# Retention and two feed-forward layers on one core: state decay on R, a new lead-in order, bursts ahead of projections, split products for the first eight units

## The chip, the core and the metric

The kernel runs on one core of one Trainium2 chip. The metric is the device time of one execution in microseconds (us). The engines are named as the profile names them: PE (TensorE, matmuls), PEld (its weight loads), DVE (VectorE), ACT (ScalarE), POOL (GpSimd) and SP (the queue that issues most DMAs). Each engine takes its instructions in the order in which the program holds them; a wait at the head of a queue holds all that stands behind it.

## What is computed

```python
# retention: B, H, S, D = 4, 8, 768, 64
for t in range(S):
    state = gamma * state + k[t]^T v[t]          # per batch and head, 64 x 64
    y[t] = scale * (q[t] @ state)
x = y as (3072, 512)
h = x @ w_in                                     # 512 -> 2048
x = (h * sigmoid(1.702 * h)) @ w_out             # 2048 -> 512
x = (sigmoid(x @ w_gate) * (x @ w_val)) @ w_out2 # 512 -> 1536 -> 512
```

## The kernel before

**Retention** goes by chunks of 128 tokens, 24 in all, six to a batch (`c = s % 6`). For chunk `s`: `emit_scores` (L137) multiplies keys by queries into two PSUM banks and DVE multiplies them by the decay mask into `A` (L148); `emit_y` (L173) adds the state's part (L178, queries scaled on POOL into `qs`, L120, times `R`) and the chunk's own part (L185, `V` times `A`), then ACT rounds the bank into `xh` (L189) and DVE subtracts the rest into `xl` (L190); `emit_update` (L152) adds `K^T vs` to the state bank `st` (L165, `vs` scaled on POOL, L112) and ACT copies it to `R` (L171). The state is kept without decay from chunk to chunk, so the queries are scaled by a table `dq` per `c`, which ACT makes in the lead-in (`emit_decays`, L125).

**The first layer** has 2048 / 128 = 16 slices of features. A *unit* is one block of 512 tokens and one slice `f`. Its projection (`proj`, L256) is 12 matmuls of 128x512: the float32 product as three products of two float32r parts (`wh*xh`, `wh*xl`, `wl*xh`). ACT and DVE make the gated value (`gated`, L263); two units later (`DEPTH`) `emit_out` (L336) adds the unit to four accumulators. For the first eight units (`i < WHOLE`) that product is four plain float32 matmuls (L352), which the profile shows as eight rows, with the gated value and the weight unsplit; from unit 8 on it is 12 float32r matmuls, for which `split_w` (L248: ACT `wh`, POOL `wl`), a cast `gh` (L275) and a subtraction `gl` (L282) make the parts. Units 0 to 7 are the first half of block 0, 8 to 15 that of block 1.

**Weights** come as 64-bit floats and are converted on the core (`convert`, L209): ACT scales both words (`cva` L222, `cvb` L224), DVE joins sign and bits (L229, L232), POOL adds (L242, `wraw`). `cvb` has two buffers. In units 0 to 7 two tiles are converted in each unit: `conv` at the unit's head, `conv2` with its ACT part at the head and its DVE and POOL parts at the unit's end, after the gated value.

**The order** is written out by hand. A unit runs: both conversions' ACT part, `conv`, projection, split of the next unit's weights, gated value, a *burst* where the table `bursts` has one (`burst`, L298: `y` and state of a chunk, scores of the next, its POOL work and loads), `conv2`, then `emit_out` of the unit before last. Projections, `y` and scores of the bursts take PSUM banks in turn from one row of three (`h`, banks 4 to 6), so a burst's `y` bank is taken again by the next projection behind the burst's two score banks. In the lead-in (L648 to L699) chunks 0 to 3 go through `retain` one after another, with conversions between them, ahead of unit 0.

Of the kernel before, what the change touches and what calls it, by code (L numbers as in the profile page):

```python
# [8 lines left out]
F32 = mybir.dt.float32  # L9
# [15 lines left out]
def retention_moe_moe2(  # L25
# [20 lines left out]
    WARM = 10  # L46
# [29 lines left out]
    dq_sb = [const.tile([P, KC, C], F32, name=f"dq{i}") for i in range(CPB - 1)]  # L76
    dv_sb = const.tile([P, CPB - 1, H], F32, name="dv_sb")
    dc_sb = const.tile([P, H], F32, name="dc_sb")
    dg_sb = const.tile([P, KC], F32, name="dg_sb")
    sig = const.tile([P, 1], F32, name="sig")  # L80
    dm_sb = const.tile([P, 2, KC, C], F32, name="dm_sb")
# [8 lines left out]
    in_t = {}  # L90
# [14 lines left out]
    def emit_prep(s):  # L105

        c = s % CPB
        q, v = in_t[s][Q], in_t[s][V]
        vs = qs = None
        if c < CPB - 1:  # L110
            vs = at_p.tile([P, H, D], F32, name="vs", tag="vs")
            nc.gpsimd.tensor_tensor(  # L112
                out=vs,
                in0=v.rearrange("p (h d) -> p h d", h=H),
                in1=dv_sb[:, c, :].unsqueeze(2).to_broadcast([P, H, D]),
                op=ALU.mult,
            )
        if c:
            qs = at_p.tile([P, KC, C], F32, name="qs", tag="qs")
            nc.gpsimd.tensor_tensor(  # L120
                out=qs, in0=q.rearrange("p (a i) -> p a i", a=KC), in1=dq_sb[c - 1], op=ALU.mult
            )
        qs_t[s], vs_t[s] = qs, vs

    def emit_decays(c):  # L125

        for a in range(KC):
            nc.scalar.mul(dq_sb[c - 1][:, a, :], dq_sb[max(c - 2, 0)][:, a, :], dg_sb[:, a:a + 1])
# [23 lines left out]
    def emit_update(s):  # L152


        c = s % CPB
        if c == CPB - 1:
            return
        if c == 0:
            state[s // CPB] = psum_tile("st", (P, KC, P))
        st = state[s // CPB]  # L160
        kn, vs = in_t[s][KN], vs_t[s]
        for hp in range(KC):
            for i in range(2):
                h = 2 * hp + i
                nc.tensor.matmul(  # L165
                    st[D * i:D * (i + 1), hp, :D], kn[:, D * h:D * (h + 1)], vs[:, h, :],
                    start=(c == 0 and hp == 0), stop=True, skip_group_check=True,
                )
        for i in range(2):
            a, b = D * i, D * (i + 1)  # L170
            nc.scalar.copy(R[(s + 1) % 2][a:b, :, a:b], st[a:b, :, :D])  # L171

    def emit_y(s, xh, xl, o):  # L173
# [16 lines left out]
        nc.vector.tensor_tensor(out=xl[:, :, o:o + C], in0=bank, in1=xh[:, :, o:o + C], op=ALU.subtract)  # L190
# [98 lines left out]
    def retain(s):  # L289

        j, i = s // 4, s % 4
        if i == 0:
            alloc_x(j)
        emit_y(s, *x_t[j], i * C)
        emit_update(s)
        del in_t[s], qs_t[s], vs_t[s]

    def burst(s):  # L298

        retain(s)  # L300
        if s + 1 < NSTEP:
            emit_scores(s + 1)
            emit_prep(s + 1)
        load_next(s + 2, Q, K, V, KN)
# [343 lines left out]
    with tc.manual_schedule():  # L648
        load_in(0, Q, in_p, "in")
        load_in(0, K, in_p, "in", nc.scalar)  # L650
        nc.sync.dma_start(out=dm_sb, in_=decay.rearrange("p (i a j) -> p i a j", i=2, a=KC))
        nc.sync.dma_start(out=dv_sb[:, 0, :], in_=dv)
        load_in(0, V, in_p, "in", nc.scalar)
        load_in(0, KN, in_p, "in", nc.scalar)
        nc.sync.dma_start(out=dg_sb, in_=dg)
        nc.sync.dma_start(out=dc_sb, in_=dv[P // 2:P // 2 + 1, :].to_broadcast([P, H]))
        nc.sync.dma_start(out=dq_sb[0], in_=dq.rearrange("p (a i) -> p a i", a=KC))
        for t in range(1, 4):
            for i in (Q, K, V):
# [20 lines left out]
        emit_decays(1)  # L680
        banks.extend(["h", "acc", "h", "acc", "h", "acc", "acc"])
        emit_prep(0)
        emit_scores(0)
        load_next(4, KN, V)
# [18 lines left out]
        for i, (b, f) in enumerate(units):  # L703
# [194 lines left out]
```

## Time and profile before

| what | value |
|---|---|
| median of 3 runs | 1178.56 us (1177.11 to 1178.95) |
| the profiled execution's own time | 1178.58 us |
| its span from first to last instruction | 1176.8 us |
| mean granted clock of TensorE | 0.997 |
| PE busy | 1163.3 us (99% of the span) |
| DVE, ACT, POOL busy | 643.5, 578.5, 559.0 us |

The profiled execution stands at the median of the runs, and its time is its span and 1.8 us around it. PE is busy nearly throughout, so one reads first where it is not, and then which of its work can shrink. Most of that is in the first 60 us.

### The profile page before, as it was taken

The page shows a single profiled execution, that of the slowest core. Times are in us where ns is not written, and L with a number is a line of the kernel's source. Part 1 is how long each engine was busy: PE and PEld are TensorE (multiplying, and loading weights), DVE is VectorE, ACT ScalarE, POOL GpSimd, SP SyncE. Part 2 cuts the span into 40 slices and gives each one's busy share as a digit, 9 for nine tenths or more (in the row PEclk, how much of TensorE's full clock was granted, in tenths as well). Part 3 has the DMA queues.
Part 4 walks back from the last instruction along what each step waited for, and adds up shares of the span by engine and source line. Part 5 has one row for each costly group of instructions (what it writes and reads, how often), then busy time and mean ns, then how long its engine had stood idle before and what let it go on. Part 6 is the DMA issues. An engine that isn't in the chain of part 4 may idle for free.

```text
span 1176.8 us, 16048 instructions
## 1 busy us (share of the span) xinstructions
PE 1163.3 (99%) x5916; PEld 953.8 (81%) x5916; DVE 643.5 (55%) x878; ACT 578.5 (49%) x1016; POOL 559.0 (48%) x434
## 2 busy tenths in 40 slices
PE   7899999999999999999999999999999999999998
PEld 7666888888888888887888888888888888888887
DVE  4755455565455455554664626377626468636454
ACT  4645665455545555454554535264526164626250
POOL 3666774334433444433454616166616167625340
PEclk8999999999999999999999999999999999999999
DMA  8664345444354333403102202042202043212111
GB/s 296 230 221 141 107 144 189 161 152 129 105 152 153 117 117 126 143 28 106 29 1 94 77 27 81 27 152 99 81 27 81 27 143 107 75 35 73 36 36 72
DMA packets 62574, 123.47 MB, mean 105 GB/s; under 512 B 6816, under 2 KB 16288, under 8 KB 62496
## 3 DMA queue, kind: packets, MB, share of 16 engines
q1 hardware_dynamic: 61920, 121.54, 31.5%
q8 instruction: 46, 0.75, 0.3%
q10 hardware_dynamic: 576, 0.92, 0.2%
q14 instruction: 32, 0.26, 0.1%
HBM read 98.31 MB, written 24.12 MB: 104 GB/s over the span
## 4 chain that ended last, share of the span: by engine, by line
PE 95%; DVE 1%; ACT 1%; DMA 1%; POOL 1%; issue 0%; SPq 0%; DVEq 0%; POOLq 0%; ACTq 0%
PE pa L503 17%; PE pd L503 8%; PE h L261 7%; PE h L259 7%; PE h L260 7%; PE acc L356 7%; PE acc L358 7%; PE acc L357 7%; PE po L625 4%; PE po L627 4%; PE pb L503 4%; PE po L626 4%; PE acc L352 2%; PE h L144 2%; PE h L185 2%; PE pd L625 1%
## 5 line engine op out<-in xcount | busy, mean ns | idle before, releaser
L252 POOL TENSOR_TENSOR wl<-wraw,wh 128x512 fp32r<-128x512 f32 x112 | 151.7, 1360 | 274.6 <-ACT wh L251 258.7
L259 PE MATMUL h<-xh,wh 128*128 128x512 f32 x384 | 153.2, 399 | 1.8 <-DVE gw L270 1.5
L270 DVE TENSOR_TENSOR sg<-h,sg 128x512 f32<-128x512 f32 x88 | 60.8, 691 | 169.0 <-ACT sg L269 168.9
L261 PE MATMUL h<-xh,wl 128*128 128x512 f32 x384 | 149.8, 390 | 0.2
L260 PE MATMUL h<-xl,wh 128*128 128x512 f32 x384 | 149.6, 389 | 0.2 <-DVE xl L190 0.2
L356 PE MATMUL acc<-gh,wh 128*128 128x512 f32 x352 | 138.9, 395 | 0.0
L357 PE MATMUL acc<-gh,wl 128*128 128x512 f32 x352 | 137.1, 390 | 0.0
L358 PE MATMUL acc<-gl,wh 128*128 128x512 f32 x352 | 137.1, 390 | 0.0
L495 POOL TENSOR_TENSOR ol<-raw,oh 128x768 fp32r<-128x768 f32 x36 | 67.0, 1861 | 124.4 <-ACT oh L492 124.4
L251 ACT CAST wh<-wraw 128x512 fp32r<-128x512 f32 x184 | 107.7, 616 | 31.2 <-PE acc L358 31.0
L269 ACT ACTIVATE sg<-h 128x512 f32<-128x512 f32 x88 | 52.6, 597 | 131.0 <-PE h L261 130.7
L503 PE MATMUL pa<-xoh,oh 128*128 128x512 f32 x288 | 112.7, 391 | 0.0
L503 PE MATMUL pa<-xol,oh 128*128 128x512 f32 x288 | 112.2, 389 | 0.0
L503 PE MATMUL pa<-xoh,ol 128*128 128x512 f32 x288 | 112.1, 389 | 0.0
L282 DVE TENSOR_TENSOR gl<-sg,gh 128x512 fp32r<-128x512 f32 x88 | 70.1, 797 | 60.4 <-ACT gh L275 60.4
L615 POOL TENSOR_TENSOR wol<-wor,woh 128x512 fp32r<-128x512 f32 x36 | 57.1, 1586 | 83.1 <-ACT woh L614 83.1
L275 ACT CAST gh<-sg 128x512 fp32r<-128x512 f32 x88 | 54.6, 621 | 71.6 <-DVE sg L270 71.6
L259 PEld LDWEIGHTS h<-xh,wh 128*128 128x128 f32 x384 | 72.1, 188 | 19.0 <-DVE gw L270 1.7
L260 PEld LDWEIGHTS h<-xl,wh 128*128 128x128 f32 x384 | 72.1, 188 | 17.1 <-issue 1.9
L261 PEld LDWEIGHTS h<-xh,wl 128*128 128x128 f32 x384 | 72.1, 188 | 16.4 <-DVE wl L252 1.0
L625 PE MATMUL po<-woh,g2h 128*128 128x512 f32 x216 | 84.0, 389 | 0.0
L626 PE MATMUL po<-wol,g2h 128*128 128x512 f32 x216 | 84.0, 389 | 0.0
(131 smaller groups left out, 2540.7 us busy)
## 6 DMA issues: line engine op xcount, KB each, us to landing
w<-in_w_dram SPq DMA_DIRECT2D x68, 512.0 KB, 3.7
in_t<-in_qkv_dram SPq DMA_DIRECT2D x93, 256.0 KB, 3.7
raw<-w2d SPq DMA_DIRECT2D x72, 256.0 KB, 3.1
w2d<-cva SPq DMA_DIRECT2D x36, 256.0 KB, 2.2
wor<-w2d SPq DMA_DIRECT2D x36, 256.0 KB, 2.6
out_dram<-ost SPq DMA_DIRECT2D x23, 256.0 KB, 2.0
xt<-x2d SPq DMA_DIRECT2D x18, 256.0 KB, 4.5
x2d<-ost SPq DMA_DIRECT2D x14, 256.0 KB, 2.7
```

The costliest lines, as they stand in the source:

```text
L251: nc.scalar.copy(wh, raw)
L252: lo_engine.tensor_tensor(out=wl, in0=raw, in1=wh, op=ALU.subtract)
L259: nc.tensor.matmul(bank[:, :n], wh[:, k, :], xh[:, k, :n], start=(k == 0), stop=False)
L260: nc.tensor.matmul(bank[:, :n], wh[:, k, :], xl[:, k, :n], start=False, stop=False)
L261: nc.tensor.matmul(bank[:, :n], wl[:, k, :], xh[:, k, :n], start=False, stop=(k == KC - 1))
L282: nc.vector.tensor_tensor(out=gl[:, :n], in0=sg[:, :n], in1=gh[:, :n], op=ALU.subtract)
L356: nc.tensor.matmul(a, wh[:, wc], gh[:, :n], start=st, stop=False)
L357: nc.tensor.matmul(a, wl[:, wc], gh[:, :n], start=False, stop=False)
L358: nc.tensor.matmul(a, wh[:, wc], gl[:, :n], start=False, stop=sp)
L503: nc.tensor.matmul(bank, w[:, kk], x[:, k, :], start=start and k == 0 and w is wh and x is xh, stop=stop and k == 1 and w is wl, skip_grou ...
L625: nc.tensor.matmul(bank, gh, wh, start=f == 0, stop=False)
L626: nc.tensor.matmul(bank, gh, wl, start=False, stop=False)
```

## The change

Names: `load_in` loads a chunk's part, `stage` loads weights to be converted, `load_next` loads parts of later chunks.

- The decay goes into the state: `R` is now made by DVE as `st` times a decay table `dg_sb` (a slice per `c`, made by four small DVE operations), so one table `dq_sb` serves all chunks, and `emit_decays` with its 20 ACT operations is gone, as are all 40 ACT copies to `R`.
- Lead-in: seven warm-up matmuls instead of ten; `A` of chunk 0 ahead of the small decay operations; scores of the next chunk ahead of the current chunk's `xl`, and for the first chunks `xl` behind them; the two conversions spread over the chunks; loads in a new order, two small ones issued by ACT.
- Bursts stand ahead of the unit's projection instead of behind its gated value, and the fourth ones of the first two rows of four are at slice 7 instead of 6.
- `WHOLE = 0`: units 0 to 7 make `gh`, `gl` and a split output weight, and their output products are 12 float32r matmuls.
- The scores of chunk 4 and the first `y` banks are taken from other rows.

```diff
-    WARM = 10
+    WARM = 7
...
-    def emit_prep(s):
+    def emit_qs(s):
...
+            nc.gpsimd.tensor_tensor(out=qs_t[s], in0=q, in1=dq_sb, op=ALU.mult)
+
+    def emit_vs(s):
...
         for i in range(2):
             a, b = D * i, D * (i + 1)
-            nc.scalar.copy(R[(s + 1) % 2][a:b, :, a:b], st[a:b, :, :D])
+            nc.vector.tensor_tensor(
+                out=R[(s + 1) % 2][a:b, :, a:b],
+                in0=st[a:b, :, :D],
+                in1=dg_sb[a:b, c, :].unsqueeze(2).to_broadcast([D, KC, D]),
+                op=ALU.mult,
+            )
...
-    def retain(s):
+    def retain(s, after=lambda: None):
...
-        emit_y(s, *x_t[j], i * C)
+        low = emit_y(s, *x_t[j], i * C)
+        if i == 3 or s >= 4:
+            low()
         emit_update(s)
-        del in_t[s], qs_t[s], vs_t[s]
+        after()
+        if i < 3 and s < 4:
+            low()
...
-    bursts = {f: 4 + n for n, f in enumerate((1, 3, 5, 6))}
-    bursts.update({3 * FH + f: 8 + n for n, f in enumerate((1, 3, 5, 6))})
+    bursts = {f: 4 + n for n, f in enumerate((1, 3, 5, 7))}
+    bursts.update({3 * FH + f: 8 + n for n, f in enumerate((1, 3, 5, 7))})
...
-    WHOLE = FH
+    WHOLE = 0
...
-        nc.sync.dma_start(out=dg_sb, in_=dg)
-        nc.sync.dma_start(out=dc_sb, in_=dv[P // 2:P // 2 + 1, :].to_broadcast([P, H]))
-        nc.sync.dma_start(out=dq_sb[0], in_=dq.rearrange("p (a i) -> p a i", a=KC))
+        nc.sync.dma_start(out=dq_sb, in_=dq.rearrange("p (a i) -> p a i", a=KC))
+        nc.scalar.dma_start(out=dg_sb[:, 0, :], in_=dg)
+        nc.scalar.dma_start(out=dc_sb, in_=dv[P // 2:P // 2 + 1, :].to_broadcast([P, H]))
...
         for t in range(4):
-            retain(t)
-            emit_decays(t + 2)
+            retain(t, lambda: emit_scores(t + 1) if t < 3 else None)
             if t < 3:
-                emit_scores(t + 1)
-                emit_prep(t + 1)
-            if t in (0, 2):
-                for step in convert(1):
-                    step()
-                stage()
-            else:
-                split_for(t // 2)
+                emit_qs(t + 1)
...
+        second[2]()
+        split_for(1)
+        stage(2)
         banks.clear()
-        banks.append("h")
+        banks.extend(["acc", "acc"])
...
             conv[1]()
             if i < FH:
                 conv[2]()
+            if i in bursts:
+                burst(bursts[i])
             hb = psum_tile("h")
             proj(hb, w_t.pop((i, 0)), xh, xl, n)
...
-            if i in bursts:
-                burst(bursts[i])
             if i >= FH:
                 conv[2]()
```

Three places in the order. The first is ACT in unit 3, the first unit with the burst of chunk 5 (`cva`, `cvb` are the conversions, the wait for Pool is for the POOL add that frees a buffer). Before:

```order
L222 ACTIVATE cva_633<-w64_577 128x512 [waits DMAHW2_49,DVE_49]
L224 ACTIVATE cvb_634<-w64_577 128x512 [waits Activation_49,Pool_49]
L251 CAST wh_656<-wraw_593 128x512
L269 ACTIVATE gw_660<-h_643 128x512 [waits PE_49]
L189 CAST xh_524<-h_663 128x4x128 [waits PE_49]
```

After:

```order
L226 ACTIVATE cva_639<-w64_567 128x512 [waits DMAHW2_49]
L228 ACTIVATE cvb_640<-w64_567 128x512 [waits Activation_49,Pool_49]
L189 CAST xh_486<-h_649 128x4x128 [waits PE_49]
L255 CAST wh_701<-wraw_583 128x512
L255 CAST wh_705<-wraw_619 128x512
L273 ACTIVATE sg_709<-h_688 128x512 [waits PE_49]
L279 CAST gh_712<-sg_709 128x512 [waits DVE_49]
```

The burst's `xh` has moved from behind the unit's gate to directly behind the second conversion's `cvb`, and a second `wh` and `gh` are new.

The second is DVE from the gate of unit 2 to the `xl` of chunk 5. Before, from the second conversion of unit 2 (tile 585) on:

```order
L270 TENSOR_TENSOR gw_612<-h_595,gw_612 128x512 [waits Activation_49]
L229 TENSOR_SCALAR cva_585<-cva_585 128x512 [waits Pool_49]
L232 SCALAR_TENSOR_TENSOR cva_585<-w64_486,cva_585 128x512 [waits DMAHW4_49,DVE_49]
L229 TENSOR_SCALAR cva_631<-cva_631 128x512 [waits Activation_49,Pool_49]
L232 SCALAR_TENSOR_TENSOR cva_631<-w64_575,cva_631 128x512 [waits DMAHW1_49,DVE_49]
L270 TENSOR_TENSOR gw_660<-h_643,gw_660 128x512 [waits Activation_49]
L190 TENSOR_TENSOR xl_525<-h_663,xh_524 128x4x128 [waits Activation_49]
```

After (the second conversion of unit 2 is tile 575):

```order
L274 TENSOR_TENSOR sg_606<-h_585,sg_606 128x512 [waits Activation_49]
L286 TENSOR_TENSOR gl_610<-sg_606,gh_609 128x512 [waits Activation_49]
L233 TENSOR_SCALAR cva_575<-cva_575 128x512 [waits Pool_49]
L236 SCALAR_TENSOR_TENSOR cva_575<-w64_468,cva_575 128x512 [waits DMAHW4_49,DVE_49]
L233 TENSOR_SCALAR cva_637<-cva_637 128x512 [waits Activation_49,Pool_49]
L236 SCALAR_TENSOR_TENSOR cva_637<-w64_565,cva_637 128x512 [waits DMAHW1_49,DVE_49]
L192 TENSOR_TENSOR xl_487<-h_649,xh_486 128x4x128 [waits Activation_49]
```

`gl`, which waits for ACT's `gh`, now stands ahead of the conversion, and the burst's `xl` ahead of unit 3's gate.

The third is DVE at the start of the lead-in. Before:

```order
L677 TENSOR_TENSOR dc_sb_121<-dc_sb_121 128x8 [waits DMAHW7_49]
L679 TENSOR_TENSOR dv_sb_120<-dv_sb_120,dc_sb_121 128x8 [waits DMAHW5_49,DVE_49]
L679 TENSOR_TENSOR dv_sb_120<-dv_sb_120,dc_sb_121 128x8 [waits DVE_49] x3
L148 TENSOR_TENSOR A_225<-h_215,dm_sb_124 128x512 [waits DMAHW2_49,PE_49]
L148 TENSOR_TENSOR A_227<-acc_216,dm_sb_124 128x512 [waits PE_49]
```

After:

```order
L143 TENSOR_TENSOR A_208<-h_198,dm_sb_121 128x512 [waits DMAHW2_49,PE_49]
L143 TENSOR_TENSOR A_210<-acc_199,dm_sb_121 128x512 [waits PE_49]
L694 TENSOR_TENSOR dg_sb_118<-dg_sb_118 128x4 [waits DMAHW6_49]
L694 TENSOR_TENSOR dg_sb_118<-dg_sb_118 128x4 [waits DVE_49] x3
L695 TENSOR_TENSOR dc_sb_117<-dc_sb_117 128x8 [waits DMAHW0_49]
L697 TENSOR_TENSOR dv_sb_116<-dv_sb_116,dc_sb_117 128x8 [waits DMAHW5_49,DVE_49]
```

`A` of chunk 0 no longer stands behind the operations that wait for a small load.

## Rows read from the trace of the kernel before

**Rows 1.** Windows: stretch, length, busy us (instructions) by engine, PE clock, DMA.

```profile
20.00:25.00 5.00, 4.30 (x44) 4.01 (x46) 0.00 (x0) 0.64 (x3) 4.10 (x4) 0.66 1.01 387
60.00:70.00 10.00, 10.00 (x55) 6.82 (x55) 4.67 (x7) 5.27 (x9) 6.58 (x7) 1.00 0.51 185
```

**Rows 2.** Timeline, lead-in: start, length, instruction, [idle before it, releaser].

```profile
1.48 4.63 PE L671 MATMUL acc<-warm 128*128 128x128 f32 x20 [1.48 <-DVE warm L668]
9.01 0.69 DVE L148 TENSOR_TENSOR A<-h,dm_sb 128x512 f32<-128x512 f32 x1
20.70 2.08 PE L178 MATMUL acc<-qs,R 128*128 128x128 f32 x8 [2.18 <-POOL qs L120]
29.77 0.50 PE L260 MATMUL h<-xl,wh 128*128 128x512 f32 x1 [0.23 <-DVE xl L190]
```

**Rows 3.** DMA issues at 1.1 to 1.2 us and 8.4 to 8.8 us: size, us to landing.

```profile
dm_sb<-in_decay_dram SPq DMA_DIRECT2D x1, 512.0 KB, 5.1
in_t<-in_qkv_dram SPq DMA_DIRECT2D x2, 256.0 KB, 5.6
```

**Rows 4.** Timeline: what follows unit 1's projection, its `cvb`, and unit 3's `xh`, `xl`.

```profile
37.98 1.05 PE L178 MATMUL h<-qs,R 128*128 128x128 f32 x8
39.78 0.70 ACT L224 ACTIVATE cvb<-w 128x512 uint32<-128x512 uint32 x1 [3.27 <-POOL wraw L242]
54.85 0.58 ACT L189 CAST xh<-h 128x512 fp32r<-128x512 f32 x1 [0.36 <-PE h L185]
55.47 0.69 DVE L190 TENSOR_TENSOR xl<-h,xh 128x512 fp32r<-128x512 f32 x1 [0.26 <-ACT xh L189]
```

**Rows 5.** Timeline of unit 7: from its gate round to POOL's add.

```profile
85.31 0.67 ACT L224 ACTIVATE cvb<-w 128x512 uint32<-128x512 uint32 x1 [2.33 <-POOL wraw L242]
85.88 0.61 ACT L251 CAST wh<-wraw 128x512 fp32r<-128x512 f32 x1
87.84 0.60 ACT L269 ACTIVATE gw<-h 128x512 f32<-128x512 f32 x1 [1.35 <-PE h L261]
88.47 0.69 DVE L270 TENSOR_TENSOR gw<-h,gw 128x512 f32<-128x512 f32 x1 [2.65 <-ACT gw L269]
89.08 0.42 DVE L229 TENSOR_SCALAR cva<-cva 128x512 uint32<-128x512 uint32 x1
89.53 0.69 DVE L232 SCALAR_TENSOR_TENSOR cva<-w,cva 128x512 uint32<-128x512 uint32 x1
90.30 1.39 POOL L242 TENSOR_TENSOR wraw<-cva,cvb 128x512 uint32<-128x512 uint32 x1 [1.80 <-DVE cva L232]
90.59 1.65 DVE L232 SCALAR_TENSOR_TENSOR cva<-w,cva 128x512 uint32<-128x512 uint32 x1
```

**Rows 6.** Timeline of unit 11, where the values are split: `gh` and `gl`.

```profile
112.47 0.69 DVE L270 TENSOR_TENSOR sg<-h,sg 128x512 f32<-128x512 f32 x1 [0.23 <-ACT sg L269]
113.20 0.62 ACT L275 CAST gh<-sg 128x512 fp32r<-128x512 f32 x1 [0.76 <-DVE sg L270]
113.85 1.35 DVE L282 TENSOR_TENSOR gl<-sg,gh 128x512 fp32r<-128x512 f32 x1 [0.69 <-ACT gh L275]
```

**Rows 7.** Chain that ended last, 76 to 106 us: start, length, what.

```profile
77.96 0.89 PE h L178 x8
78.85 1.02 PE h L185 x16
79.88 0.46 PE st L165 x16
80.34 1.09 PE h L144 x16
...
85.06 0.23 PE h L259
...
87.81 3.43 PE acc L352 x8
...
103.57 0.23 PE h L259
```

More of the change, by code (lines that the diff above doesn't have):

```diff
@@ L73, in psum_tile @@
         return psum[i].tile(list(shape), F32, name=kind, tag="bank")
-    dq_sb = [const.tile([P, KC, C], F32, name=f"dq{i}") for i in range(CPB - 1)]
+    dq_sb = const.tile([P, KC, C], F32, name="dq_sb")
     dv_sb = const.tile([P, CPB - 1, H], F32, name="dv_sb")
     dc_sb = const.tile([P, H], F32, name="dc_sb")
-    dg_sb = const.tile([P, KC], F32, name="dg_sb")
+    dg_sb = const.tile([P, CPB - 1, KC], F32, name="dg_sb")
     sig = const.tile([P, 1], F32, name="sig")
+    const.tile([P, 16], F32, name="pad")
     dm_sb = const.tile([P, 2, KC, C], F32, name="dm_sb")
@@ L117, in emit_prep @@
             )
[L118 to L128, printed above, removed]
     A_t = {}
@@ L189, in emit_y, with low @@
         nc.scalar.copy(xh[:, :, o:o + C], bank)
-        nc.vector.tensor_tensor(out=xl[:, :, o:o + C], in0=bank, in1=xh[:, :, o:o + C], op=ALU.subtract)
+        def low():
+            nc.vector.tensor_tensor(out=xl[:, :, o:o + C], in0=bank, in1=xh[:, :, o:o + C], op=ALU.subtract)
+        return low
     raw1 = {}
@@ L293, in retain @@
             alloc_x(j)
-        emit_y(s, *x_t[j], i * C)
+        low = emit_y(s, *x_t[j], i * C)
+        if i == 3 or s >= 4:
+            low()
         emit_update(s)
-        del in_t[s], qs_t[s], vs_t[s]
+        after()
+        if i < 3 and s < 4:
+            low()
+        for t in (in_t, qs_t, vs_t):
+            t.pop(s, None)
     def burst(s):
@@ L302, in burst @@
             emit_scores(s + 1)
-            emit_prep(s + 1)
+            emit_qs(s + 1)
+            emit_vs(s + 1)
         load_next(s + 2, Q, K, V, KN)
@@ L671, in retention_moe_moe2 @@
             nc.tensor.matmul(warm_ps[:, :P], warm[:, :P], warm[:, :P], start=True, stop=True)
-        stage(1)
-        load_next(4, Q, K)
         for r in R:
             nc.vector.memset(r, 0.0)
+        banks.extend(["h", "acc", "h", "acc", "h", "acc", "acc"])
+        emit_scores(0)
+        emit_vs(0)
+        load_next(4, V, KN)
+        for c in range(1, CPB - 1):
+            nc.vector.tensor_tensor(out=dg_sb[:, c, :], in0=dg_sb[:, c - 1, :], in1=dg_sb[:, 0, :], op=ALU.mult)
         nc.vector.tensor_tensor(out=dc_sb, in0=dc_sb, in1=dc_sb, op=ALU.mult)
@@ L679, in retention_moe_moe2 @@
             nc.vector.tensor_tensor(out=dv_sb[:, c, :], in0=dv_sb[:, c - 1, :], in1=dc_sb, op=ALU.mult)
[L680 to L684, printed above, removed]
+        first = second = None
         for t in range(4):
-            retain(t)
-            emit_decays(t + 2)
+            retain(t, lambda: emit_scores(t + 1) if t < 3 else None)
             if t < 3:
-                emit_scores(t + 1)
-                emit_prep(t + 1)
-            if t in (0, 2):
-                for step in convert(1):
-                    step()
-                stage()
-            else:
-                split_for(t // 2)
-        load_next(5, Q, K)
+                emit_qs(t + 1)
+            if t == 0:
+                load_next(5, Q, K)
+                first = convert(1)
+                first[0]()
+            elif t == 1:
+                first[1]()
+            elif t == 2:
+                first[2]()
+                second = convert(1)
+                second[0]()
+            if t < 3:
+                emit_vs(t + 1)
+            if t == 2:
+                split_for(0)
+                second[1]()
+        second[2]()
+        split_for(1)
+        stage(2)
         banks.clear()
-        banks.append("h")
+        banks.extend(["acc", "acc"])
         pend = deque()
@@ L735, in retention_moe_moe2 @@
                 emit_scores(4)
-                emit_prep(4)
+                emit_qs(4)
+                emit_vs(4)
                 load_next(5, V, KN)
-            if i in bursts:
-                burst(bursts[i])
+                banks.clear()
+                banks.append("h")
             if i >= FH:
```

23 lines of the change are left out of this document (14 added, 9 removed).

## The prediction

> **What bounds the kernel now.** I read the windows first: from 60 us on PE is busy in every microsecond at the full clock (the row at 60 to 70 stands for the later ones), so what happens before that reaches the end only as a shift, and what PE no longer has to do comes off in full. Before 60 us there are holes, and the clock falls with them: 0.66 granted in 20 to 25 us [rows 1]. The timeline then says what ends the holes: in the lead-in a small load ahead of `A` and a late `qs`; the first projection gets its `xl` at 29.77 us [rows 2]. In units 0 to 3 it is the conversion: ACT's `cvb` stood 3.27 us for a buffer that POOL's add frees [rows 4]. By unit 4 PE has become the slowest, and the chain of waits runs on PE alone [rows 7]. So the question is where the end of unit 7's projection, and of the output product of unit 7 (103.57 us, [rows 7]), will stand.
>
> **Output products.** A whole product of a unit takes 3.43 us on PE. A projection is also 12 split matmuls and lasts 87.81 - 85.06 = 2.75 us [rows 7], so the split product takes 2.75 too: 0.68 less, eight times, **-5.4 us on PE** if nothing else waits. It adds in each unit on ACT a `wh` (0.61, [rows 5]) and a `gh` (0.62), on DVE a `gl` (0.69, as the multiply, if nothing hinders it; 1.35 in [rows 6], where it met POOL), on POOL a `wl` (about 1.3, as long as the add [rows 5]).
>
> **Lead-in.** The ten warm-up matmuls (20 rows) last 4.63 us from 1.48; seven end 1.3 us earlier, at 4.8, but `A` of chunk 0 needs the mask, which landed at 1.18 + 5.1 = 6.3 [rows 2, 3]. So `A` starts at about 6.7 instead of 9.01. The new limit is the loads: the keys of chunk 2 were issued at about 8.5 and took 5.6 us [rows 3], so its scores can't start before 14.1. From there PE has scores 1.09, `y` 0.89 + 1.02, update 0.46 and the scores of chunk 3, 1.09 [rows 7], and waits some 0.4 for `A`: 19.1. Two `A` at 0.65 make 20.4, the last `y` (1.02) 21.5, `xh` (0.58, [rows 4]) 22.1. `xl` stands on DVE behind an older `xl` and a conversion, one part of which meets POOL (1.65 instead of 0.69, [rows 5]); the conversion ends at 23.0, `xl` at 23.7: 23.7 against 29.77, **6.1 us earlier**. Bounds: 3 if the loads of chunk 2 land 3 us later, 7 if POOL doesn't hold DVE up. The decay on `R` costs DVE two operations of half a partition set from PSUM; no row shows them, ACT's copies of that form are shorter than an `xl` (0.69), so between 0 and 0.7 for both, 0.7 taken; they are inside this sum. ACT's 20 decay operations no longer stand there; they had cover from the waits for loads.
>
> **Units 0 and 1.** Here the lead is spent. ACT reaches unit 0's gate at 27.3, since it comes behind a `wh` (0.61) and four conversion steps at 0.57, which start when POOL has added the second converted weight at 24.4 (23.0 + 1.4). From the gate on: 0.63 to the multiply, 0.73 to `gh`, 0.65 to `gl` [rows 5, 6]; `gl` 0.61, which meets POOL's `qs` (+0.4), two `A` 1.3, a conversion 1.15, POOL's add 1.4, then `cvb` 0.57, `xh` 0.6, `xl` 0.75: 36.1. Only then may unit 1's projection start, because burst 4 now stands ahead of it and its `y` bank is the projection's. It ends at **38.8; before 37.98** [rows 4]. The burst is done by then, which before it was not.
>
> **Units 2 to 7.** Each step of this loop is in [rows 4 to 6]. After an odd unit's projection: gate to multiply 0.63, multiply to `gh` 0.73, to `gl` 0.65, to DVE's shift 0.61 (the step from multiply to shift in [rows 5]), to its join 0.45, to POOL's add 0.77, add 1.42, `cvb` 0.57, two `wh` 1.14: **6.97 us to the next gate**. In the even unit the same up to the add (5.26), then `cvb` 0.57, `xh` 0.62, `xl` 0.75: **7.20 us to the odd unit's projection**, which takes 2.78. Sum 16.95, and 0.3 for POOL's adds drawn out by DVE, 17.3 for two units. Before, the three pairs from 37.98 to 87.81 [rows 4, 7] took 16.6 each, and there PE was the limit. PE's own work in the pairs is now 11.3, 13.6 and 14.5: 4 x 2.75 + 3.46 in the last, without the state's product in the second, without update and one output product in the first. It will stand still for 6.0, 3.7 and 2.8 us, most of it just ahead of the odd projection. So the saving of the split products goes into the wait of `xh` behind `cvb`. Three pairs: 38.8 + 51.9 = 90.7 against 87.81. Behind it PE has five pieces of 2.75, 104.4 against 103.57: **+0.9 us**.
>
> **The clock.** In the trace a hole of 2.2 us ahead of 20.70 [rows 2] was followed by a stretch at 1.2 GHz: eight L178 rows took 2.08 us instead of 0.89 [rows 2, 7], and 20 to 25 had 0.66 granted [rows 1]. The new holes are 6.0, 3.7 and 2.8 us. A projection at half the clock would take up to 2.75 us more; none is in the trace. Between 0 and 2.75 each; I take half, 1.4, for the first two and 0.4 for the third, as the hole of 20.70, after which L178 lost 1.2 us, is nearest: **+3.2 us**. It delays the next gate, so nothing hides it.
>
> **Later bursts.** There are 16 more. From the end of `y` to the projection it is `xh` 0.62 and `xl` 0.75, and 0.46 + 1.09 of PE work stands between [rows 4, 7], which covers it. Where a batch ends there is no update, 0.3 us is bare, three times: **+0.9 us**. Before, the output product gave cover here; if DVE were not free it would be up to 0.6 each, 9.6 in all. ACT is freed of the copies to `R`; it has idle time there, so 0.
>
> **The sum**, against the profiled execution's 1178.58 us (which is the median of the runs to 0.02): +0.9 + 3.2 + 0.9 = +5.0, **1183.6 us**.
>
> **The DVE-POOL collisions.** L232 lasts 0.69 alone and 1.65 where POOL's add has begun just before it [rows 5]; `gl`, with two SBUF inputs too, took 1.35 [rows 6]. [...]
>
> **Rivals.**
> 1. *Faster: the queue ahead hides the wait.* If POOL's add came back before the burst's `y` ends, the pairs would run at PE's own work: 6.0 + 3.7 + 2.8 = 12.5 less and no clock loss (3.2): 1167.9. For it: PE was the limit from unit 4 on [rows 7]. Against it: the steps of the loop are all in rows, and they add to 16.95. It turns faster by over 0.2% (2.4 us, about what a measurement of this kernel tells from no change) if a pair takes under 15.9 us without clock loss (0.9 + 0.9 - 3 x 1.4 = -2.4). Chance 0.12.
> 2. *Same: the loop as I have it, but the clock stays up.* 1180.4. It is the sum without the 3.2. For it: the only row with a hole and its clock is from the lead-in, with short matmuls around it; against it: two of the new holes are longer than that one. Chance 0.22.
> 3. *Slower still: collisions.* Each of the six links pays 1.65 - 0.69 = 0.96: +5.8, 1189.4. For it: POOL gets busier; against it: at the point where `gl` starts POOL's two `wl` have just ended. Chance 0.12.
> 4. *The lead-in gives only 3 us* because the loads land late: 1186.7. Chance 0.06.
>
> My forecast has 0.48, with a range of its own of 1181 to 1187.
>
> **How the numbers follow.** Slower by over 0.2% is above 1180.9: nearly all of the forecast (0.46), rivals 3 and 4: 0.64. Same: rival 2 and the forecast's lower edge: 0.24. Faster: rival 1: 0.12. The range leaves out rival 1 and the upper edge of rival 3, whose collisions could cost more than one each: 1177 to 1190.
>
> **What would show it.** In the profile after: the first `xl` matmul near 24 us (step 1); `cvb` waiting for POOL's add in every unit up to 7, and the bursts' `xh` right behind it; holes of PE ahead of the projections of units 3, 5, 7 that end with DVE's `xl`; a granted clock under 1 after them; the output product of unit 7 ending at 105 to 108 us. If PE is full from 45 us on, the loop was wrong; if the holes are there at full clock, only the clock was; if later bursts show idle PE, the 0.9 was too small.

## The result and the profile after

The changed kernel takes 1194.7 us (median of four runs, 1192.4 to 1196.9) against 1178.2 us: a ratio of 1.0144, with a 95% interval of 1.0126 to 1.0162. It is slower, as forecast, but by 16.5 us and not by 5.0, outside the range. The profiled execution is the slowest of the four: 1196.85 us, span 1195.1 us (before 1176.8), mean granted clock 0.991 (before 0.997).

I compare the two traces by the time at which PE goes on behind a projection. Where the changed kernel stands behind the one before:

| PE is at | behind by, us | forecast |
|---|---|---|
| the end of unit 10's projection (steady from here to unit 24) | 12.5 | 4.1 (0.9 + 3.2) |
| the last projection (unit 95) | 17.9 | 5.0 |
| the end of the span | 18.3 | 5.0 |

So 12.5 us are lost before 120 us, 5.4 us at a few places between units 24 and 70, and 0.4 us in the second layer. (These are of the profiled executions; the medians lie 16.5 us apart.)

Windows of the changed kernel (columns as in [rows 1], which they answer; the clock column is the one after POOL's):

```profile
20.00:25.00 5.00, 3.82 (x51) 3.09 (x49) 4.92 (x8) 2.44 (x4) 3.51 (x3) 1.00 1.04 408
...
50.00:55.00 5.00, 0.88 (x14) 0.69 (x12) 4.32 (x5) 2.79 (x6) 2.62 (x3) 0.98 0.31 87
55.00:60.00 5.00, 3.85 (x9) 3.08 (x10) 1.89 (x3) 1.40 (x3) 4.63 (x4) 0.50 0.97 350
60.00:65.00 5.00, 5.00 (x20) 3.98 (x20) 1.98 (x4) 2.57 (x5) 0.00 (x0) 0.84 0.05 20
75.00:80.00 5.00, 3.57 (x8) 2.81 (x9) 2.75 (x6) 1.69 (x4) 4.84 (x5) 0.53 0.86 310
95.00:100.00 5.00, 3.27 (x8) 2.60 (x9) 3.02 (x6) 1.99 (x4) 4.57 (x4) 0.57 0.81 238
```

From 50 to 55 us PE is busy 0.88 us of 5, and then does nine matmuls in 3.85 us at a granted clock of 0.50, the 1.2 GHz level. The same comes back at 75 and 95 us. The clock drop of the lead-in [rows 1] is gone in this trace. Timeline of the changed kernel around unit 3, which answers [rows 4 to 6] (start, length, instruction, [idle before it, releaser]):

```profile
48.62 2.51 POOL L256 TENSOR_TENSOR wl<-wraw,wh 128x512 fp32r<-128x512 f32 x2
...
50.36 1.32 DVE L286 TENSOR_TENSOR gl<-sg,gh 128x512 fp32r<-128x512 f32 x1 [0.68 <-ACT gh L279]
...
52.82 1.37 POOL L246 TENSOR_TENSOR wraw<-cva,cvb 128x512 uint32<-128x512 uint32 x1 [1.69 <-DVE cva L236]
...
54.23 0.67 ACT L228 ACTIVATE cvb<-w 128x512 uint32<-128x512 uint32 x1 [2.21 <-POOL wraw L246]
54.80 0.57 ACT L189 CAST xh<-h 128x512 fp32r<-128x512 f32 x1
...
55.40 0.69 DVE L192 TENSOR_TENSOR xl<-h,xh 128x512 fp32r<-128x512 f32 x1 [0.66 <-ACT xh L189]
...
56.15 0.79 PE L263 MATMUL h<-xh,wh 128*128 128x512 f32 x1 [5.26 <-DVE xl L192]
...
61.67 0.60 ACT L273 ACTIVATE sg<-h 128x512 f32<-128x512 f32 x1 [5.27 <-PE h L265]
```

This is the chain that the prediction describes: `gl` (drawn out from 0.69 to 1.32 us by POOL's `wl`), the conversion, POOL's add, `cvb` that waits for it, `xh` right behind `cvb`, `xl`, and only then the projection, after 5.26 us of idle PE. The other two holes, and the gate of unit 7:

```profile
76.43 0.79 PE L263 MATMUL h<-xh,wh 128*128 128x512 f32 x1 [3.96 <-DVE xl L192]
...
96.73 0.80 PE L263 MATMUL h<-xh,wh 128*128 128x512 f32 x1 [3.02 <-DVE xl L192]
...
102.25 0.60 ACT L273 ACTIVATE sg<-h 128x512 f32<-128x512 f32 x1 [5.27 <-PE h L265]
```

The holes are 5.26, 3.96 and 3.02 us; the forecast was 6.0, 3.7 and 2.8. From the projection's first matmul to the gate it takes 5.52 us each time, where unit 1, at the full clock, took 3.05 (38.39 to 41.44).

In the chain that ended last the row that answers to the last one of [rows 7] (103.57, forecast 105 to 108):

```profile
116.07 0.23 PE h L263
```

The lead-in, answering [rows 2, 5]:

```profile
18.81 1.65 DVE L236 SCALAR_TENSOR_TENSOR cva<-w,cva 128x512 uint32<-128x512 uint32 x1
...
23.07 1.32 DVE L233 TENSOR_SCALAR cva<-cva 128x512 uint32<-128x512 uint32 x1
...
25.77 0.50 PE L264 MATMUL h<-xl,wh 128*128 128x512 f32 x1 [0.91 <-DVE xl L192]
...
38.39 0.50 PE L263 MATMUL h<-xh,wh 128*128 128x512 f32 x1 [1.78 <-DVE xl L192]
```

The first `xl` matmul is 4.0 us earlier than the 29.77 of [rows 2], not 6.1; unit 1's projection starts at 38.39, forecast 36.1.

### The profile page after: what moved, and what is told of

Its sections match the earlier page's. It is cut to its first block, busy times and chain, and to the rows that moved or that the text cites. A ratio compares the mean times of both kernels' runs of the same rounds, so it can differ in the third digit from the quotient of the medians.

```text
span 1195.1 us, 16098 instructions
## 1 busy us (share of the span) xinstructions
PE 1163.2 (97%) x5942; PEld 961.7 (80%) x5942; DVE 688.8 (58%) x930; ACT 567.3 (47%) x972; POOL 575.3 (48%) x442
## 4 chain that ended last, share of the span: by engine, by line
PE 89%; DVE 4%; ACT 3%; DMA 2%; issue 1%; POOL 1%; SPq 0%; ACTq 0%; DVEq 0%; POOLq 0%
PE pa L514 16%; PE pd L514 8%; PE h L263 7%; PE h L265 7%; PE h L264 7%; PE acc L367 6%; PE acc L368 6%; PE acc L369 6%; PE po L638 4%; PE po L636 4%; PE po L637 4%; PE pb L514 4%; PE pd L638 1%; PE pd L636 1%; PE pd L637 1%; PE h L185 1%
## 5 line engine op out<-in xcount | busy, mean ns | idle before, releaser
L256 POOL TENSOR_TENSOR wl<-wraw,wh 128x512 fp32r<-128x512 f32 x120 | 162.4, 1361 | 269.1 <-ACT wh L255 259.2
L263 PE MATMUL h<-xh,wh 128*128 128x512 f32 x384 | 155.2, 404 | 16.5 <-DVE xl L192 15.2
L367 PE MATMUL acc<-gh,wh 128*128 128x512 f32 x384 | 150.3, 391 | 1.5 <-DVE ost L386 1.5
L368 PE MATMUL acc<-gh,wl 128*128 128x512 f32 x384 | 149.5, 389 | 0.0
L369 PE MATMUL acc<-gl,wh 128*128 128x512 f32 x384 | 149.4, 389 | 0.0
L274 DVE TENSOR_TENSOR sg<-h,sg 128x512 f32<-128x512 f32 x96 | 66.3, 691 | 143.2 <-ACT sg L273 143.2
L273 ACT ACTIVATE sg<-h 128x512 f32<-128x512 f32 x96 | 57.4, 598 | 155.8 <-PE h L265 155.4
L286 DVE TENSOR_TENSOR gl<-sg,gh 128x512 fp32r<-128x512 f32 x96 | 85.4, 889 | 65.9 <-ACT gh L279 65.9
L279 ACT CAST gh<-sg 128x512 fp32r<-128x512 f32 x96 | 59.6, 620 | 80.7 <-DVE sg L274 80.7
L265 PEld LDWEIGHTS h<-xh,wl 128*128 128x128 f32 x384 | 73.8, 192 | 17.3 <-DVE wl L256 1.5
L367 PEld LDWEIGHTS acc<-gh,wh 128*128 128x128 f32 x384 | 72.5, 189 | 18.0 <-DVE ost L386 2.7
L369 PEld LDWEIGHTS acc<-gl,wh 128*128 128x128 f32 x384 | 72.2, 188 | 15.2
```

Source lines behind the costliest of these rows:

```text
L256: lo_engine.tensor_tensor(out=wl, in0=raw, in1=wh, op=ALU.subtract)
L263: nc.tensor.matmul(bank[:, :n], wh[:, k, :], xh[:, k, :n], start=(k == 0), stop=False)
L265: nc.tensor.matmul(bank[:, :n], wl[:, k, :], xh[:, k, :n], start=False, stop=(k == KC - 1))
L274: nc.vector.tensor_tensor(out=sg[:, :n], in0=bank[:, :n], in1=sg[:, :n], op=ALU.mult)
L286: nc.vector.tensor_tensor(out=gl[:, :n], in0=sg[:, :n], in1=gh[:, :n], op=ALU.subtract)
L367: nc.tensor.matmul(a, wh[:, wc], gh[:, :n], start=st, stop=False)
```

## The experiments

Two parts of the change carry the loss, the place of the bursts and the split products. E1, E4 and E6 give the four combinations, all with the new lead-in and the decay on `R`; the columns hold the bursts of the later units too (medians, us):

| | bursts behind the gated value | bursts ahead of the projection |
|---|---|---|
| whole products in units 0 to 7 | 1174.7 (E6) | 1181.5 (E4) |
| split products | 1183.9 (E1) | 1194.7 (the changed kernel) |

**E1, bursts back.**

```diff
-            if i in bursts:
-                burst(bursts[i])
             hb = psum_tile("h")
...
+            if i in bursts:
+                burst(bursts[i])
             if i >= FH:
```

> The changed kernel with every burst back behind the gated value, at slices 1, 3, 5, 6; lead-in, decay on R and split products stay. Theory (the burst ahead of the projection puts its xh on ACT behind cvb, which waits for POOL's add, and the projection of the odd unit waits for it): the holes of PE ahead of the projections of units 3, 5, 7 and their three stretches at half the clock go, unit 1's projection no longer waits for xl (38.4 -> 31 to 33 us), and the 5.4 us lost between unit 24 and 70 come back: 1166 to 1177 us. Rival (the split products make the loop of conversions too long wherever the burst stands): holes of the same sum at other places, 1185 or more.

Measured: 1183.9 us, 1.0057 (1.0038 to 1.0076). 10.8 of the 16.5 us come back, and unit 1's projection starts at 29.41. But the time is above the theory's range: the projections of units 3, 5 and 7 don't wait for `xl` any more, and PE now waits for gates in the middle of the bursts. What PE waited for from 20 to 120 us in E1 (us in total, times, longest; L139 are the scores of a burst, L274 is the gate's multiply):

```profile
PE h L139 <- DVE sg L274: 7.4, 4, 3.5
PE h L263 <- DVE xl L192: 1.0, 1, 1.0
```

The longest of these was followed by a projection of unit 2 that took 5.3 us. So the rival has a share: with split products the loop is too long at the bursts' old place as well, and unit 7's projection ends 3.2 us later than before in spite of a lead of 5.7 at unit 1.

**E2, a third buffer for `cvb`.**

```diff
-            b = cv_p.tile([P, 512], U32, name="cvb", tag="cvb")
+            b = cv_p.tile([P, 512], U32, name="cvb", tag="cvb", bufs=3)
```

> The changed kernel with three buffers for cvb instead of two, so that no cvb waits for the POOL add of the unit before; nothing else is changed. Theory: it is this wait alone that xh stands behind; the projections of units 3, 5, 7 start when PE has done what stands ahead of them, no half clock, unit 7's projection ends near 82 us instead of 102, 1174.5 us (1172 to 1180). The 5.4 us of the later units stay lost. Rival (DVE and POOL are the bound by their own work): the wait moves to another place of the same loop, unit 7's projection ends after 95 us, 1188 or more.

Measured: 1187.1 us, 1.0086 (1.0071 to 1.0101). The time is near the rival's; unit 7's projection ends at 91.7 us, between the theory's 82 and the rival's 95. Timeline of E2 around unit 3:

```profile
49.30 0.57 ACT L189 CAST xh<-h 128x512 fp32r<-128x512 f32 x1
...
50.60 1.38 POOL L246 TENSOR_TENSOR wraw<-cva,cvb 128x512 uint32<-128x512 uint32 x1 [1.08 <-DVE cva L236]
...
50.89 1.63 DVE L236 SCALAR_TENSOR_TENSOR cva<-w,cva 128x512 uint32<-128x512 uint32 x1
52.45 0.68 DVE L192 TENSOR_TENSOR xl<-h,xh 128x512 fp32r<-128x512 f32 x1
...
53.18 0.80 PE L263 MATMUL h<-xh,wh 128*128 128x512 f32 x1 [5.40 <-DVE xl L192]
...
71.45 0.50 PE L263 MATMUL h<-xh,wh 128*128 128x512 f32 x1 [3.15 <-DVE xl L192]
```

`xh` no longer waits, and ends 2.6 us before `xl` starts: `xl` stands on DVE behind two conversions, one of them drawn out by POOL's add. So the wait of `cvb` was one of two that end almost together (in the changed kernel DVE was done with the same conversions at 54.74 us, 0.6 us before `xh` ended); without it the other holds the projection up. From the gate of unit 3 (57.59) to that of unit 5 (74.51) it still takes 16.9 us. The time fell by 7.6 us, for the most part through the clock: only the first hole was followed by a slow projection, of 4.4 us, which is 1.4 us lost instead of 7.4.

**E3, zeros in the holes.**

```diff
                 burst(bursts[i])
+                if 1 < i < FH:
+                    for k in range(14):
+                        bank = acc_t[0][k % 4]
+                        nc.tensor.matmul(bank, zero, x_t[0][0][:, 0, :], start=False, stop=False)
             hb = psum_tile("h")
```

> The changed kernel with 14 float32r matmuls of 128x512 that add zeros to the accumulators (3.2 us at full clock) ahead of the projections of units 3, 5 and 7, inside the holes of 4 to 5.3 us; the sums are unchanged. Theory (the hole costs the clock, and the clock costs the projection): the three projections take 2.75 us instead of 5.3, the holes themselves stay in length, 1187 us, 7.6 less than the changed kernel. Rival (these projections are slow for another reason, such as operands that arrive late): they stay at 5.3 us, 1194.7.

Measured: 1187.2 us, 1.0087 (1.0069 to 1.0105), as the theory had it. Windows of E3, and its timeline (its line numbers are one higher here):

```profile
50.00:55.00 5.00, 4.38 (x28) 3.34 (x28) 4.34 (x5) 2.77 (x6) 2.63 (x2) 1.00 0.22 73
55.00:60.00 5.00, 3.72 (x16) 3.11 (x17) 1.93 (x4) 2.13 (x5) 4.77 (x4) 1.00 0.99 375
```

```profile
50.91 3.47 PE L755 MATMUL acc<-xh,zero 128*128 128x512 f32 x14
...
56.28 0.50 PE L264 MATMUL h<-xh,wh 128*128 128x512 f32 x1 [1.90 <-DVE xl L193]
...
59.33 0.60 ACT L274 ACTIVATE sg<-h 128x512 f32<-128x512 f32 x1 [2.80 <-PE h L266]
```

The projection starts at the same time (56.28 against 56.15), and its gate comes after 3.05 us instead of 5.52. Work that computes nothing makes the kernel 7.5 us faster, because it keeps the clock up. This isolates the clock's share.

**E4, whole products.** `WHOLE = FH` instead of 0, nothing else.

> The changed kernel with whole float32 output products in units 0 to 7 as before (no gh, gl, second wh, wl there); bursts stay ahead. Theory: gh and gl (0.73 + 0.65 us in each unit) and a wh (0.57) leave the loop, a pair falls by some 3 us from 20.3, while PE has 0.68 us more in each unit: the holes shrink to 1 to 2 us. If the half clock stays 1187, if it goes 1180. Rival (the split products don't lengthen the loop): only PE's 5.4 us come on top, 1200.

Measured: 1181.5 us, 1.0026 (1.0015 to 1.0037), near the theory's 1180. Of the three holes one is left (2.38 us, ahead of unit 3's projection, part of which ran at half the clock). Splitting the eight products, which saves PE 0.68 us in each, costs 13.2 us with the bursts ahead (against the changed kernel) and 9.2 with them behind (E1 against E6).

**E5, later bursts back.** The bursts of units 24 on behind the gated value, those of units 1 to 7 ahead.

```diff
+            if i in bursts and i < FH:
...
+            if i in bursts and i >= FH:
+                burst(bursts[i])
```

> The changed kernel with the bursts of units 24 on back behind the gated value (slices 1, 3, 5, 6 for the first four); those of units 1 to 7 stay ahead of the projection. Theory (with the burst ahead, nothing of PE stands between a projection and the output product that ends a block, so the copies of the accumulators come on DVE behind the gate and gl, their stores go out later, and PE waits for the accumulator): of the 5.4 us that the trace of the changed kernel loses between units 24 and 70 some 4.2 come back, 1190.5 us; 1.2 stay, as with all bursts back. Rival (the loss comes from the decay on R, which puts two more operations on DVE in each burst): 1194.7.

Measured: 1191.0 us, 1.0105 (1.009 to 1.012). The median fits the theory, the trace only by half. Between units 24 and 70 E5 falls back by 2.7 us instead of 5.4; E1, which has the same order there, by 1.2. The difference stands at one block end, where DVE waits 4.36 us for a store in E5 and 2.53 in E1 (see E12). Most of the rest of what E5's profiled execution is faster stands ahead of unit 24: its third hole (3.14 us) was not followed by the half clock.

**E6, lead-in and decay on `R` alone.** E1 and E4 together.

> Only the lead-in and the decay on R of the change: bursts back behind the gated value, whole float32 products in units 0 to 7. Theory: unit 1's projection starts at 29.4 us instead of 35.1, the loop of conversions takes some 2.5 us of this back up to unit 4, the decay on R in each burst 0.85 us of DVE, from where on PE is full: 1176.5 us (1174 to 1180), slightly faster than before. Rival (the lead is lost entirely in the loop, whose pairs are as long as before): the end of unit 7's projection at 87.8 us or later, 1178.5 to 1181.

Measured: 1174.7 us, 0.9969 (0.9957 to 0.9981): faster than both kernels, near the theory. The first projection ends 3.3 us earlier than before, unit 7's 3.0 us earlier, and from 60 us on PE is full. No run separates the lead-in from the decay on `R`.

**E7, `gl` behind the second conversion.**

```diff
-            gated_lo(g_t[i], n)
+            if i >= FH:
+                gated_lo(g_t[i], n)
...
             for step in conv2[1:]:
                 step()
+            if i < FH:
+                gated_lo(g_t[i], n)
```

> The changed kernel with gl of units 0 to 7 behind the unit's second conversion on DVE instead of ahead of it; bursts stay ahead. Theory (each step of the loop from gate to gate counts in full): 0.65 us of gl in each unit and some 0.7 of its collision with POOL in each pair leave the loop, a pair takes 18.3 us instead of 20.3 if the half clock stays: 1188.7 us; down to 1182 if the shorter holes don't cost the clock. Rival (POOL is behind anyway, and the conversion waits for its wl): 1194.

Measured: 1189.6 us, 1.009 (1.0075 to 1.0105), near the theory in time, but by another sum. The projections of units 3, 5 and 7 start 18.4 and 19.0 us apart instead of 20.3; 18.3 was expected. The rest is the clock: the hole ahead of unit 7 has shrunk to 1.53 us, and its projection took 3.06 us to the gate, the time at full clock.

**E8, all three at once.** Three `cvb` buffers, `gl` behind, later bursts back, and the bursts of units 1 to 7 at the unit's head:

```diff
+            if i in bursts and i < FH:
+                burst(bursts[i])
             conv[0]()
             conv2[0]()
             conv[1]()
```

> The changed kernel with the three things that hold up the projection taken away at once: the bursts of units 1 to 7 at the unit's head, ahead of both conversions on ACT and DVE; three buffers for cvb; gl behind the second conversion; later bursts back behind the gated value. Theory: xh and xl stand behind nothing but their own y, the loop from gate to gate falls to some 5 us for a unit, less than PE's own work, PE is full from unit 2 on, unit 7's projection ends at 77 to 81 us: 1168 us (1164 to 1175). Rival (DVE and POOL can't convert two tiles in a unit any faster): unit 7's projection after 87 us, 1180 or more.

Measured: 1180.2 us, 1.0019 (1.0009 to 1.0028). The rival: with the three things taken away the pairs still take 15.7 and 16.9 us, and unit 7's projection ends at 86.7 us. Groups of E8 from 40 to 90 us (line, operation, count | busy us, mean ns):

```profile
L236 DVE SCALAR_TENSOR_TENSOR cva<-w,cva 128x512 uint32<-128x512 uint32 x13 | 15.7, 1211 | 0.4
L233 DVE TENSOR_SCALAR cva<-cva 128x512 uint32<-128x512 uint32 x12 | 13.3, 1111 | 0.0
L286 DVE TENSOR_TENSOR gl<-sg,gh 128x512 fp32r<-128x512 f32 x6 | 8.4, 1405 | 0.0
...
L256 POOL TENSOR_TENSOR wl<-wraw,wh 128x512 fp32r<-128x512 f32 x13 | 19.6, 1524 | 0.0
```

In these 50 us DVE is busy for 46.3, POOL for 41.8 and PE for 44.6. DVE has operations that take 0.69 and 0.42 us alone ([rows 5]; `gl` 0.69, as the multiply there). Here the mean is 1.21, 1.11 and 1.41. DVE and POOL hold each other up, and DVE, so drawn out, is busier than PE.

**E9, E6 with three `cvb` buffers.** The diff of E2.

> Lead-in and decay on R alone (bursts behind, whole products in units 0 to 7), with three buffers for cvb. Theory: what is left of idle PE there, 2.5 us ahead of 38.5 us and the 3.4 us at half the clock behind it (1.7 us lost), comes from the gate of unit 1, which stands on ACT behind a cvb that waits for POOL's add; with a third buffer both go: 1171 us against 1174.7. Rival (the wait moves on to a wh that waits for the same add, or to DVE): 1174.7.

Measured: 1173.9 us, 0.9963 (0.9949 to 0.9976): the fastest of the versions that compute the whole product, but not to be told from E6 by its interval, and so the rival's 1174.7 is not excluded. In the traces unit 7's projection ends 5.6 us earlier than before, against 3.0 in E6; a stretch at half the clock, behind 1.2 us of wait for a gate, is left.

**E10, E6 with units 4 to 7 split.** `WHOLE = 4`.

> Lead-in and decay on R alone, bursts behind, but whole products only in units 0 to 3; units 4 to 7 split. Theory (a split product takes from PE 0.68 us and gives POOL a wl and DVE a gl, which pay only where those have time to spare; from unit 4 on PE is full, POOL 61 to 68% and DVE 65 to 70% busy): part of the 2.7 us is gained, 1173 us (1172 to 1175). Rival (as with all eight split, where it cost 9.2 us, each split unit costs time on the loop, some 1.1 us each): 1179.

Measured: 1175.4 us, 0.9976 (0.9966 to 0.9986). Between the two: against E6's 1174.7 it neither gains nor loses, so the gain that the theory expected is not there. Where PE is already the limit the split costs about as much as it saves.

**E11, E8 without the output weights' low part.**

```diff
+            if j < FH:
+                wh = wsp_p.tile([P, 512], F32R, name="wh", tag="wh")
+                nc.scalar.copy(wh, raw1[units[j][1], 1])
+                w_t[j, "out"] = wh, wh
+                return
```

> The kernel with bursts at the unit's head, three cvb buffers and gl behind the conversion, without the low part wl of the output weights of units 0 to 7: their products use wh in its place, so PE's work is the same and POOL's falls by one wl (1.27 us) in each unit. Theory (what is left there is POOL and DVE holding each other up: DVE 98% busy at 40 to 50 us, its join 1.65 us instead of 0.69): DVE's joins get shorter, a pair falls from 16.3 us to PE's own 14.5, 1173 us. Rival (the order of DVE's queue is the limit, whatever POOL does): 1180.

Measured: 1173.6 us, 0.9958 (0.9944 to 0.9972), 6.6 us faster than E8; the time is the theory's. The kernel leaves out a term of the product, so it is a probe and not a version to use. The pairs take 13.7 and 15.0 us. The groups of E11 that answer to those of E8:

```profile
L236 DVE SCALAR_TENSOR_TENSOR cva<-w,cva 128x512 uint32<-128x512 uint32 x14 | 16.4, 1175 | 0.5
L233 DVE TENSOR_SCALAR cva<-cva 128x512 uint32<-128x512 uint32 x14 | 12.9, 924 | 0.0
...
L286 DVE TENSOR_TENSOR gl<-sg,gh 128x512 fp32r<-128x512 f32 x7 | 4.8, 679 | 0.0
```

`gl` is back at its own 0.68 us; the joins, which the theory named, are hardly shorter. So it was `gl` against `wl` that gave way, and POOL's own 1.27 us.

**E12, copies ahead of the gate at block ends.** `late` is true in units 33, 49 and 65.

```diff
-            g_t[i] = gated(hb, n, i < WHOLE)
-            gated_lo(g_t[i], n)
+            if not late:
+                g_t[i] = gated(hb, n, i < WHOLE)
+                gated_lo(g_t[i], n)
...
                 emit_out(pend.popleft())
+            if late:
+                g_t[i] = gated(hb, n, i < WHOLE)
+                gated_lo(g_t[i], n)
```

> The changed kernel, bursts ahead everywhere, but in the three units whose burst meets the end of a block (units 33, 49, 65) the copies of the accumulators stand ahead of the unit's gate and gl on ACT and DVE instead of behind them. Theory (the late copies hold up the stores, and these the next block's accumulators): from unit 47 to 72 the changed kernel fell back by 5.0 us against before (shift of the projections from 12.8 to 17.9); of this the 1.5 us wait for ost, the 1.0 us for wh behind it and the half of what follows go, 2.5 to 3.5 us: 1191.7 us. Rival (the stores take as long whenever they start, so the wait stays): 1194.7; or the gate, now behind copies that wait for stores, holds PE up: 1196 or more.

Measured: 1194.1 us, 1.0131 (1.0113 to 1.0148): the rival. From unit 47 to 72 its trace falls back by 4.5 us, the changed kernel's by 5.0. `ost` holds the copy of an accumulator until its store (to `x2d`) has gone out. First the changed kernel at the end of block 2, then E12:

```profile
366.02 0.69 DVE L386 COPY ost<-acc 128x512 f32<-128x512 f32 x1
370.88 0.69 DVE L386 COPY ost<-acc 128x512 f32<-128x512 f32 x1 [4.17 <-DMA x2d<-ost]
371.47 0.59 ACT L384 COPY ost<-acc 128x512 f32<-128x512 f32 x1 [5.61 <-DMA x2d<-ost]
...
371.62 0.50 PE L367 MATMUL acc<-gh,wh 128*128 128x512 f32 x1 [1.52 <-DVE ost L386]
...
373.73 0.50 PE L263 MATMUL h<-xh,wh 128*128 128x512 f32 x1 [0.45 <-ACT wh L255]
```

```profile
362.84 0.69 DVE L386 COPY ost<-acc 128x512 f32<-128x512 f32 x1 [1.18 <-PE acc L369]
366.20 0.69 DVE L386 COPY ost<-acc 128x512 f32<-128x512 f32 x1 [2.67 <-DMA x2d<-ost]
...
368.04 0.59 ACT L384 COPY ost<-acc 128x512 f32<-128x512 f32 x1 [3.93 <-DMA x2d<-ost]
...
372.19 0.50 PE L263 MATMUL h<-xh,wh 128*128 128x512 f32 x1 [1.91 <-ACT wh L255]
```

The wait for the accumulator is gone. In its place ACT's copy, which waits for a store, holds the next `wh` up, and PE waits 1.9 us for that. DVE stood 4.17 us for a store in the changed kernel, 2.67 in E12. That this wait is shorter can't be put down to the new order: at this block end it is, in the traces of all runs, either 2.5 to 2.7 us (before, E1, E3, E4, E6, E8 to E12) or 4.2 to 4.5 (the changed kernel, E2, E5, E7), with the bursts ahead or back. Why stays open. E4 is the fairer comparison: it has the changed kernel's order and the short wait (2.54 us), no wait for the accumulator, and PE waits 0.65 us for `wh`. This block end costs 1.55 us there and 2.5 in E12, so by these traces the new order makes it worse.

## Why the prediction was wrong in size

**Right.** The direction; the mechanism and its place; the holes to within 0.8 us each; the loop without gain. Unit 1's own steps were right too: its projection came 2.3 us late, and 2.1 of that is the lead-in's. The later bursts' bare `xl` cost 1.3 us in the shift of the two traces, against 0.9, but only in part where I had put it. At two ends of a batch PE waits 0.32 us, as forecast; behind the third, chunk 23, no scores follow, and there is no wait. The third wait, 0.56 us, is in the middle of a batch (unit 69), where the conversion on DVE is drawn out beside POOL (L233 1.49 us, L236 1.41) and `xl` comes late.

**The clock, 3.2 forecast, 7.4 measured.** This is the largest error, 4.2 us, and the step of the sum that failed most. I had bounded a projection's loss by 0 and 2.75 and took half for two holes and 0.4 for the third, after a row with short matmuls. Each of the three lost 5.52 - 3.05 = 2.47 us. E3 confirms it: the same holes with zeros in them, 7.5 us less. The upper bound was the value to take, and rival 2 (the clock stays up) fell.

**The loop, 17.3 forecast, 17.8 measured.** From gate to gate (41.44, 61.67, 81.95, 102.25) a pair took 20.2 to 20.3 us, less 2.47 for the clock 17.8. From an odd unit's gate to the next gate it took 6.9 us, as forecast (6.97); in the even unit the way to the odd projection took 7.8 to 7.9 instead of 7.20. That is `gl` of the even unit, 1.32, 1.39 and 1.37 instead of 0.69. From the projection's start to its gate it took 3.05 at the full clock instead of 2.78, which about uses up the 0.3 that I had allowed for POOL's adds. I had noted the meeting in [rows 6], but wrote that POOL's two `wl` have then just ended; they had not (48.62 + 2.51 = 51.13, `gl` started at 50.36). So rival 3 was half true, in three links of six; the three pairs took 1.5 us more than forecast.

The Trainium skill ("SBUF — State Buffer", Who interferes with whom) says that a VectorE instruction with two SBUF inputs contends with a GpSimd instruction that reads SBUF, and the trace agrees: `gl` and `wl` are of this kind, and `gl` took up to 1.39 us beside `wl`. The same section of the Trainium skill names `tensor_scalar` among the operations that can contend in a two-port mode. L233, a `tensor_scalar` with one input, took 1.32 us at 23.07 in the changed kernel and 1.11 on average in E8, instead of 0.42; which mode it ran in the traces don't show. For an instruction with at most one SBUF input, outside such a mode, the same section of the Trainium skill says that it does not contend, and the trace agrees on the decay on `R`, which reads its other input from PSUM: each of its 40 operations took 0.40 to 0.43 us. The two together, 0.85 us, are above the 0.7 that I had as their upper bound.

**The lead-in, 6.1 forecast, 4.0 measured.** The scores of chunk 2 started at 15.39 us, when their load had landed, and not at 14.1: 1.3 us. The conversion met POOL's `qs` at 18.81 (L236 1.65 us); one such meeting I had charged. A second came at 23.07, beside POOL's `wl` (L233 1.32 us instead of 0.42). In the runs with this lead-in the first projection starts between 22.6 and 25.1 us. Rival 4 (3 us, late loads) was nearer than my sum, and right about the loads; 2.1 us of error.

**A term that was missing: ends of blocks, 4.1 us.** My sum had nothing for them. With the burst ahead nothing of PE stands any more between a projection and the product that ends a block, so the gate and `gl` come on DVE ahead of the copies of the accumulators. I counted the cover that the output product gave to the burst's `xl`, not the cover that the burst gave in its old place. Two block ends cost 2.9 and 1.2 us in the trace of the changed kernel. Not all of this is the bursts' place. Where the wait for the store is short (E12), the first of the two costs 1.55 us with the bursts ahead (E3, E4) and 0.5 to 0.8 with them back (E1, E6, E8 to E11); where it is long, 2.9 to 4.1 ahead (the changed kernel, E2, E7) and 2.3 back (E5). So some 1.4 of the 2.9 us go with the long wait, whose cause is open. At the second block end it is 1.1 to 1.2 us ahead (the changed kernel, E2 to E4, E7) and 0.2 to 0.6 back. How the moved burst costs the rest is argued from the order; E12, which changed the order of the copies, did not win it back.

Sum of the errors: 4.2 + 1.5 + 2.1 + 4.1 = 11.9 of 18.3 - 5.0 = 13.3; the rest is 0.4 for the later `xl`, 0.4 in the second layer, and 0.6 for unit 1 and rounding. All of them go the same way, so no term hid another.

**The question behind it**, why split products that save PE 5.4 us cost 9 to 13, is answered by E2, E8 and E11. My sum held one chain, through `cvb`, as if it were the cause. It was one of several of nearly the same length. Without it DVE's queue came next (E2), and with no queue in the way DVE, drawn out by POOL, was nearly full (E8), until a POOL operation was left out (E11). Rival 1, the only way to a gain, fell with it.

## What to carry to other kernels

Before work is moved from the busiest engine to two that share something, add up these two over the same stretch, with their drawn-out durations; where they come out longer than the busiest engine, the saving turns into holes. A hole ahead of a long row of matmuls can cost the hole and, at half the clock, nearly the row once more (here 2.47 us on 3.05): take the whole row as the price, and fill the hole if it can't be closed. When a block of work is moved, ask what it covered at its old place.

## What the runs showed that was not expected

Whether the clock fell did not follow from a hole's length alone. Holes of 5.26, 3.96 and 3.02 us in the changed kernel were each followed by a projection at 1.2 GHz, and so was one of 2.76 us in E7 (unit 5); a hole of 3.15 us in E2, also ahead of unit 5, and one of 3.14 us in E5 (unit 7) were not. The plainest pair is E12 and E5, whose programs are the same up to unit 24: ahead of unit 7's projection the one has a hole of 3.12 us and the other one of 3.14, and only the first was followed by the half clock. First E7, then E12, then E5:

```profile
72.69 0.79 PE L263 MATMUL h<-xh,wh 128*128 128x512 f32 x1 [2.76 <-DVE xl L192]
```

```profile
95.69 0.80 PE L263 MATMUL h<-xh,wh 128*128 128x512 f32 x1 [3.12 <-DVE xl L192]
```

```profile
95.21 0.50 PE L263 MATMUL h<-xh,wh 128*128 128x512 f32 x1 [3.14 <-DVE xl L192]
```

The first matmul takes 0.79 and 0.80 us in the first two and 0.50 in the third; from there to the gate it is 5.53, 5.53 and 3.07 us. This, and waits for a store that are either about 2.6 or about 4.3 us long, are where I see runs of one kernel differ by up to 4.5 us; that is argued from single traces, not shown by repeated ones.
